# Retention attention into a routed expert layer: expert 0's token list read in place of a replicated one, and half of each gate's first step moved one tile earlier

## The chip, the cores and the metric

The kernel runs on one core of a Trainium2 chip. The metric is the device time of one execution in microseconds (us), and lower is better. A core has five engines that run side by side, each its own instruction queue in order: TensorE (PE in the profile; PEld is its weight loads), VectorE (DVE), ScalarE (ACT), GpSimd (POOL) and SyncE (SP). SyncE here only issues transfers; GpSimd issues the indirect ones (gather and scatter by a list of row numbers). They wait for one another, and for transfers (DMA), through semaphores.

## The reference

Retention attention over 8 batches of 8 heads, 576 positions and head size 64, without a softmax; its output, one row of 512 numbers for each of 4608 tokens, goes through a layer of 8 experts, of which each token uses the one with the largest logit:

```python
scores = scale * np.matmul(q, k.transpose(0, 1, 3, 2))
Dmat = np.where(rel >= 0, gamma[:, None, None] ** rel[None, :, :], 0.0)
ret = np.matmul(scores * Dmat[None], v)
x = ret.transpose(0, 2, 1, 3).reshape(B * S, H * D)

logits = x @ w_gate
e_idx = np.argmax(logits, axis=1)
gate_w = softmax(logits)[np.arange(N), e_idx]
eom = 1.0 / (1.0 + np.exp(-(x @ w_output_gate)))
for e in range(E):
    mask = e_idx == e
    h = np.maximum(x[mask] @ w1[e], 0.0)
    out[mask] = gate_w[mask, None] * eom[mask, e, None] * (h @ w2[e])
```

## The kernel before

**Order.** The whole program stands under a hand-made schedule: each engine executes its instructions in the order in which the Python code issues them. An operation that is written earlier stands earlier in its engine's queue, and everything behind it on that engine waits while it waits. Only the semaphores join the engines.

**The loop** runs over 36 tiles `g` of 128 tokens (nine make two batches). For a tile, `scores(g + 1)` makes the next tile's products of q and k on TensorE, and VectorE masks them into `S_sb` (two operations of 128x512, line 389). `out_x(g)` adds the carried state's part (line 416) and the tile's own part (line 420) into the PSUM tile `o_ps`, of which there is one. From it ScalarE copies `xT` (line 428), x with the features on the partitions, and `x_rows(g)` on VectorE (line 437) transposes x into rows, which SyncE stores to `xs` in DRAM two tiles later (`store_x`). So the next tile's `out_x` cannot begin before `x_rows` has emptied `o_ps`. `update` carries the state on (line 402), `k_rows` transposes k (line 363). GpSimd scales q and v (`prep_q`, `prep_v`, lines 351 and 356), and SyncE loads the packed q, k and v (`pk`) five tiles ahead.

**The gate** runs once for four tiles; `n` numbers these groups, `late` is the tile's place behind its group, 0 to 3. At the end of the tile of late 0, `logits` (line 448) makes the group's logits on TensorE. In the next tile (late 1) `gate_a` finds each token's expert with eight operations on VectorE (a transposition, line 454, and seven small ones up to line 475), ahead of that tile's `out_x` and `x_rows`. At late 2, `ranks` on TensorE and `gate_b` on VectorE turn this into a slot in the expert's list, with `gate_d` (the rounding to `sli`, line 512) at the tile's end; at late 3 `gate_c` makes the list's entries (`meta`, lines 527 to 532), and over the next tiles GpSimd scatters them (`some`, line 536), 64 bytes for each token (its number and its weight) into the list `lst` in DRAM. The last group's gate runs after the loop.

**The experts** follow the loop. Expert `e` takes up to 616 tokens in two parts (`NS` = 360 and 256). `mm1(e, part, fb)` makes one block of 128 hidden features (12 products: the three of a split into high and low halves, by four blocks of 128 input features, line 250), `mm2(e, t)` one tile of output rows (line 266). Weights are split into a high half by ScalarE (`upper`, line 160) and a low half by VectorE (`lower`, line 165).

**Lists.** `load_idx` brings an expert's list entries into SBUF, each of them four times, for the four groups of 32 partitions. `make_idx` on VectorE makes two things from that: `gidx`, row numbers for gathers of quarter rows (line 307), and `idx`, row number and weight for whole rows (four copies, line 311). Part 0 of expert 0 is special: its list is taken from the first 24 tiles' tokens (`SNAP` = 5 is the last group counted), loaded at the end of tile 29, and its rows are gathered in tiles 31 and 32 (`gather_rows`, line 199, into a free `pk` buffer), transposed on TensorE in tile 34 (line 229), and split at tile 35, so that `mm1(0, 0, 0)` starts right behind the loop. The lines of the loop that hold this:

```python
        if g == 31:
            make_idx(0, 2, 0)
        if g + 1 < NTILE:
            prep_v(g + 1)
        if 30 < g < 33:
            for t in (0, 1) if g == 31 else (2,):
                gather_rows(t)
```

Of the kernel before, what the change touches and what calls it, by code (L numbers as in the profile page):

```python
# [38 lines left out]
GT = 4  # L39
NG = NTILE // GT  # L40
# [7 lines left out]
LW, LE = 16, 640  # L48
# [3 lines left out]
def tile_retention_moe(  # L52
# [42 lines left out]
    bump = const.tile([P, 2], F32, name="bump")  # L95
    toks = const.tile([P, NTILE, 1], I32, name="toks")
    meta = [const.tile([P, GT, LW], I32, name=f"meta{i}") for i in range(2)]
    lists0 = const.tile([P, 2, TA * 4, LW], I32, name="lists0")
    idx = const.tile([P, E, CT, 2], I32, name="idx")
    gidx = const.tile([P, E, CT * 4], I32, name="gidx")  # L100
    quad = csm_sb[:, 16:17]
# [56 lines left out]
    def upper(which, e, fp, st):  # L158
        hi = w_of(which, f"w{which}h{fp}")
        A.copy(out=hi, in_=st)  # L160
        return which, e, fp, st, hi
# [28 lines left out]
    def gather_rows(t, dep=None):  # L190

        if t == 0:
            rows = ld.tile([P, 3, 512], F32, name="pk")
            for i in range(TA):
                XG[0, i] = rows[:, i]
# [3 lines left out]
        after(G.indirect_dma_start(out=XG[0, t], out_offset=None, in_=xs[0:n, :],  # L199
                                   in_offset=bass.IndirectOffsetOnAxis(ap=idx[:, 0, t, 0:1], axis=0),  # L200
                                   bounds_check=n - 1, oob_is_err=False), dep)

    def where(t):
        part = 0 if t < TA else 1
        t0 = t - part * TA
        return part, P * t0, min(P, NS[part] - P * t0)

    def xt_of(e, part):
        if (e, part) not in XT:
# [3 lines left out]
        return XT[e, part]  # L213

    def split_x(e, t, src):
        part, c0, n = where(t)
# [10 lines left out]
    def transp_pe(t, src):  # L227
        for k in range(KB):
            T.transpose(src[:, k, :], XG[0, t][:, P * k:P * k + P], ident)
        return split_x(0, t, src)  # L230

    def transp(e, t):
# [23 lines left out]
        return done  # L256

    def mm2(e, t, between={}):
        part, c0, n = where(t)
# [11 lines left out]
        A.activation(out=y, in_=ps, func=AF.Copy, scale=idx.bitcast(F32)[0:n, e, t, 1:2])  # L271
        G.indirect_dma_start(out=out, out_offset=bass.IndirectOffsetOnAxis(ap=idx[0:n, e, t, 0:1], axis=0),  # L272
                             in_=y, in_offset=None, bounds_check=NT - 1, oob_is_err=False)

    lists1 = []

    def load_idx(e0, e1, part):
        s0, t0, nb = part * NS[0], part * 4 * TA, NB[part]

        rest = NS[part] > 32 * nb  # L280
        lists = lists0 if (e0, part) == (0, 0) else lists1[0]
        view = lst[0:E * NT, :].rearrange("(e a s) w -> e a s w", e=E, a=1)
        dmas = []
        if e1 - e0 < 4:

            for e in range(e0, e1):
                v = view[e, :, s0:s0 + 32 * nb].rearrange("a (j t) w -> a j (t w)", t=nb).broadcast_to([4, 32, LW * nb])
                dmas.append(SP.dma_start(out=lists[:, e, t0:t0 + nb].rearrange("p t w -> p (t w)"), in_=v))
                if rest:
                    v = view[e, :, s0 + 32 * nb:s0 + 32 * nb + 32].broadcast_to([4, 32, LW])  # L290
                    dmas.append(SP.dma_start(out=lists[:, e, t0 + nb], in_=v))
        for a in range(4):
            if e1 - e0 >= 4:
                v = view[e0:e1, 0, s0:s0 + 32 * nb].rearrange("e (j t) w -> j e (t w)", t=nb)
                dmas.append(SP.dma_start(out=lists[32 * a:32 * a + 32, e0:e1, t0:t0 + nb].rearrange("j e t w -> j e (t w)"),
                                         in_=v))
                if rest:
                    v = view[e0:e1, 0, s0 + 32 * nb:s0 + 32 * nb + 32].rearrange("e j w -> j e w")
                    dmas.append(SP.dma_start(out=lists[32 * a:32 * a + 32, e0:e1, t0 + nb], in_=v))
        for i in dmas:  # L300
            for j in scat:
                tc.add_manual_dep(i.ins, j.name, SYNC, reason="reads the list after every scatter so far")

    def make_idx(e0, e1, part):
        n, t0 = (TA, 0) if part == 0 else (CT - TA, TA)
        lists = lists0 if (e0, part) == (0, 0) else lists1[0]
        V.tensor_scalar(out=gidx[:, e0:e1, 4 * t0:4 * (t0 + n)], in0=lists[:, e0:e1, 4 * t0:4 * (t0 + n), 0],
                        scalar1=4.0, scalar2=quad, op0=ALU.mult, op1=ALU.add)
        for a in range(4):
            q = slice(32 * a, 32 * a + 32)  # L310
            V.tensor_copy(idx[q, e0:e1, t0:t0 + n],
                          lists[q, e0:e1].rearrange("j e (t u) w -> j e t u w", u=4)[:, :, t0:t0 + n, a, 0:2])
# [131 lines left out]
    def logits(n, ps):  # L444

        for k in range(KB):
            for q in range(GT):
                T.matmul(ps[32 * q:32 * q + 32, 0:P], lhsT=wg_sb[:, k, :], rhs=xT[n][:, q, k, :],
                         start=(k == 0), stop=(k == KB - 1), skip_group_check=True)

    def gate_a(n):
# [116 lines left out]
    for g in range(NTILE):  # L568
# [313 lines left out]
```

## Time and profile before

| what | us |
|---|---|
| median of 3 runs | 605.94 (604.21 to 612.22) |
| the profiled execution | 606.38 |
| its span, first to last instruction | 604.6 |
| TensorE busy | 576.1 (95% of the span) |
| VectorE, GpSimd, ScalarE busy | 327.7, 315.6, 169.7 |

The loop takes the span's first 155 us or so, and the experts the rest. A row of the timeline has the start, the duration, the engine, the line of the kernel, the operation, what it writes and from what, its shape, how many instructions stand in it, and in brackets how long the engine was idle before it and what released it. In the windows the columns are the length, busy time of the five engines with their instruction counts, the granted TensorE clock as a share of the full one, the share of the 16 DMA engines' time in use, and GB/s. A row of the waits has the engine, what it was to run, what it waited for, and the time: in total, how often, and the longest. The releaser is inferred: it is the last of the things waited for that left an event.

TensorE's busy time in the loop by periods of four tiles, from one gate's first `x_rows` to the next one's:

```profile
31.70:47.35 15.65, 15.01 (x354) 12.62 (x346) 10.98 (x32) 5.56 (x15) 10.63 (x13) 1.00 0.99 317
47.35:62.85 15.50, 14.80 (x375) 12.75 (x373) 10.96 (x32) 5.68 (x14) 13.55 (x17) 1.00 0.92 277
...
92.91:108.31 15.40, 15.29 (x395) 13.47 (x396) 11.08 (x32) 6.49 (x17) 13.53 (x17) 1.00 0.90 285
108.31:125.10 16.79, 15.09 (x341) 12.28 (x339) 11.07 (x35) 4.96 (x13) 14.06 (x19) 1.00 0.85 260
```

### The profile page before, as it was taken

The numbers are of one execution on the slowest core, as the hardware profiler recorded it, in microseconds if no ns is written. First come the engines' busy times: TensorE is split into PE (matmuls) and PEld (weight loads), VectorE is DVE, ScalarE is ACT, GpSimd is POOL, SyncE is SP. The second block draws the span as 40 slices with busy tenths as digits, with TensorE's granted clock in tenths as the row PEclk, the third lists the DMA queues.
The fourth block names the chain that finished last, engine by engine and source line by source line (L and its number), as shares of the span: only waits on it lengthen the run. The fifth ranks groups of instructions, "written<-read, shape, count | busy, mean of one in ns | idle before, by whom it ended". The sixth has DMA issues, their size and how long they took to land. (4 is left out here: it accounts for less than half of the span.)

```text
span 604.6 us, 14060 instructions
## 1 busy us (share of the span) xinstructions
PE 576.1 (95%) x5737; PEld 507.2 (84%) x5737; DVE 327.7 (54%) x655; ACT 169.7 (28%) x360; POOL 315.6 (52%) x333
## 2 busy tenths in 40 slices
PE   7999999888798999999999999999999999999995
PEld 4888888777696889779978997998899799889974
DVE  3566777674661869736732961584186249426300
ACT  5434334333341222132212221222222222212210
POOL 4768898867276734363553455446344535540011
PEclk9999999998999999999999999999999999999998
DMA  8999899877646436323621642262155216321001
GB/s 304 297 321 287 275 277 292 250 212 237 175 116 214 123 127 225 93 89 114 200 98 58 192 149 75 81 232 96 48 179 165 82 53 218 118 68 52 1 36 44
DMA packets 53324, 94.78 MB, mean 157 GB/s; under 512 B 9018, under 2 KB 30971, under 8 KB 53258
## 3 DMA queue, kind: packets, MB, share of 16 engines
q1 hardware_dynamic: 43594, 73.03, 38.2%
q0 software_dynamic: 9232, 20.23, 10.3%
q8 instruction: 46, 0.75, 0.5%
q10 hardware_dynamic: 432, 0.59, 0.3%
q14 instruction: 20, 0.16, 0.1%
HBM read 74.33 MB, written 20.15 MB: 156 GB/s over the span
## 5 line engine op out<-in xcount | busy, mean ns | idle before, releaser
L186 POOL DMA_INDIRECT x_q<-xs,gidx x140 | 148.7, 1062 | 113.2 <-ACT hh L254 70.9
L250 PE MATMUL h_ps<-xh,w1h 128*128 128x360 f32 (+1 forms) x512 | 154.6, 302 | 2.6 <-issue 1.3
L250 PE MATMUL h_ps<-xl,w1h 128*128 128x360 f32 (+1 forms) x512 | 154.6, 302 | 0.3 <-issue 0.3
L250 PE MATMUL h_ps<-xh,w1l 128*128 128x360 f32 (+1 forms) x512 | 154.5, 302 | 0.0
L266 PE MATMUL y_ps<-w2h,hh 128*128 128x512 f32 (+1 forms) x320 | 125.2, 391 | 2.4 <-ACT y L271 1.4
L266 PE MATMUL y_ps<-w2h,hl 128*128 128x512 f32 (+1 forms) x320 | 124.9, 390 | 0.5 <-DVE hl L255 0.5
L266 PE MATMUL y_ps<-w2l,hh 128*128 128x512 f32 (+1 forms) x320 | 124.8, 390 | 0.0
L272 POOL DMA_INDIRECT out_dram<-y,idx x40 | 41.1, 1028 | 122.6 <-ACT y L271 111.9
L250 PEld LDWEIGHTS h_ps<-xh,w1h 128*128 128x128 f32 x512 | 96.1, 188 | 3.5 <-issue 1.8
L250 PEld LDWEIGHTS h_ps<-xh,w1l 128*128 128x128 f32 x512 | 97.1, 190 | 0.2 <-issue 0.2
L250 PEld LDWEIGHTS h_ps<-xl,w1h 128*128 128x128 f32 x512 | 96.1, 188 | 1.1 <-issue 0.5
L254 ACT ACTIVATE hh<-h_ps 128x360 fp32r<-128x360 f32 (+1 forms) x128 | 54.5, 429 | 149.5 <-PE h_ps L250 126.6
L255 DVE SCALAR_TENSOR_TENSOR hl<-h_ps,hh 128x360 fp32r<-128x360 f32 (+1 forms) x128 | 58.6, 474 | 69.0 <-ACT hh L254 58.2
L266 PEld LDWEIGHTS y_ps<-w2h,hh 128*128 128x128 f32 (+1 forms) x320 | 58.8, 184 | 16.6 <-ACT y L271 1.8
L266 PEld LDWEIGHTS y_ps<-w2h,hl 128*128 128x128 f32 (+1 forms) x320 | 58.8, 184 | 15.3 <-DVE hl L255 1.3
L266 PEld LDWEIGHTS y_ps<-w2l,hh 128*128 128x128 f32 (+1 forms) x320 | 58.8, 184 | 13.4
L271 ACT ACTIVATE y<-y_ps,idx 128x512 f32<-128x512 f32 (+1 forms) x40 | 27.5, 689 | 129.7 <-issue 75.3
L389 DVE TENSOR_TENSOR S_sb<-sc,cmat_sb 128x512 f32<-128x512 f32 x72 | 46.1, 681 | 32.2 <-PE sc L385 29.6
L223 DVE TENSOR_TENSOR xl<-x_t,xh 128x512 fp32r<-128x512 f32 (+1 forms) x35 | 23.5, 672 | 63.9 <-ACT xh L220 61.9
L351 POOL TENSOR_TENSOR qs<-pk,gq_sb 128x512 f32<-128x512 f32 x36 | 46.2, 1282 | 13.4 <-DMA pk<-in_pack_dram 6.6
L536 POOL DMA_INDIRECT lst<-meta,sli x36 | 36.1, 1004 | 27.1 <-DVE meta L532 15.6
L420 PE MATMUL o_ps<-S_sb,vs 128*64 128x128 f32 x576 | 40.4, 281 | 1.8 <-DVE xq L437 0.7
(126 smaller groups left out, 604.3 us busy)
## 6 DMA issues: line engine op xcount, KB each, us to landing
st<-in_w_dram SPq DMA_DIRECT2D x61, 512.0 KB
pk<-in_pack_dram SPq DMA_DIRECT2D x31, 512.0 KB
pk<-in_pack_dram SPq DMA_DIRECT2D x35, 256.0 KB
xs<-xq SPq DMA_DIRECT2D x40, 128.0 KB
pk<-in_pack_dram SPq DMA_DIRECT2D x3, 768.0 KB
x_q<-xs,gidx POOLq DMA_INDIRECT x140
xs<-w2h SPq DMA_DIRECT2D x16, 128.0 KB
xs<-w2l SPq DMA_DIRECT2D x16, 128.0 KB
```

Source lines behind the costliest of these rows:

```text
L186: after(G.indirect_dma_start(out=XG[e, t][:, u, :], out_offset=None, in_=xs.rearrange("t (a c) -> (t a) c", a=4), in_offset=bass.IndirectO ...
L223: V.tensor_tensor(out=lo, in0=src[:, :, 0:n], in1=hi.bitcast(F32), op=ALU.subtract)
L250: T.matmul(ps, lhsT=a[:, k, :], rhs=b[:, k, :], start=(j == 0), stop=(j == 3 * KB - 1))
L254: done = A.activation(out=hh, in_=ps, func=AF.Relu)
L255: V.scalar_tensor_tensor(out=hl, in0=ps, scalar=0.0, in1=hh.bitcast(F32), op0=ALU.max, op1=ALU.subtract)
L266: i = T.matmul(ps, lhsT=a[:, c0:c0 + n], rhs=b, start=(j == 0), stop=(j == 3 * FB - 1))
L271: A.activation(out=y, in_=ps, func=AF.Copy, scale=idx.bitcast(F32)[0:n, e, t, 1:2])
L272: G.indirect_dma_start(out=out, out_offset=bass.IndirectOffsetOnAxis(ap=idx[0:n, e, t, 0:1], axis=0), in_=y, in_offset=None, bounds_check= ...
L351: G.tensor_tensor(out=qs[g], in0=pk[g][:, 0].rearrange("p (n i) -> p n i", n=NP), in1=gq_sb[:, c % 5], op=ALU.mult)
L389: V.tensor_tensor(out=S_sb[:, r].rearrange("p (a b) i -> p a b i", a=2), in0=sc[r].rearrange("p (a b) i -> p a b i", a=2), in1=m, op=ALU.mult)
L420: last = T.matmul(part(p, r), lhsT=vs[g][:, 2 * p + r, :], rhs=S_sb[:, r, p, :], start=(state is None and p < 2), stop=True, skip_group_ch ...
L536: i = G.indirect_dma_start(out=lst, out_offset=bass.IndirectOffsetOnAxis(ap=sli[:, t, :], axis=0), in_=m[:, t, :], in_offset=None)
```

## The change

1. **Expert 0's list.** `load_rows(part)` brings the list of expert 0 as it lies in DRAM: one transfer in which each partition gets the entries of its own rows. The rows' numbers and weights are used where they lie (`entry`), without an operation on VectorE. Part 0's three tiles hold 120 rows each (`N0`) instead of 128, 128 and 104, so that 360 entries divide evenly. `make_idx(0, 2, 0)` goes from tile 31, and `make_idx(0, 2, 1)` from the experts.
2. **Gathers.** Tile 31 issues one of the three gathers, tile 32 the other two; before it was two and one.
3. **Expert 1's list**, which was loaded beside expert 0's, is loaded at the end of tile 32; its `make_idx(1, 2, 0)` follows the loop, before `mm1(0, 0, 3)`. The remaining lists are loaded and made in other groups: `load_idx(1, E, 1)`, `load_idx(2, E, 0)`.
4. **The gate.** `gate_a`'s first four operations follow `logits` at the end of the tile of late 0; the other four (`gate_e`) stay where all eight were.
5. **Weight casts.** Of the first expert's four casts of w1 on ScalarE, one stands at the end of tile 33 and three after the loop; before, tiles 33, 34 and 35 had one each and one came after the loop.

On VectorE, at a gate inside the loop (group 6, tiles 28 and 29; the others are alike), before; `S_sb` is the masked scores, `lg_ps` the gate's PSUM tile, and L437 is `x_rows`:

```order
L437 STREAM_TRANSPOSE w2h_2310<-o_ps 128x4x4x32
L389 TENSOR_TENSOR S_sb<-sc_132,cmat_sb 128x512
L389 TENSOR_TENSOR S_sb<-sc_133,cmat_sb 128x512
L454 STREAM_TRANSPOSE lg_ps<-lg_ps 128x128
L458 TENSOR_REDUCE mx<-lg_ps 128x4
L459 TENSOR_TENSOR lg_ps<-lg_ps,mx 128x32
L461 TENSOR_TENSOR lm<-lg_ps,mx 128x32
L462 TENSOR_TENSOR lg_ps<-lg_ps,csm_sb 128x32
L464 TENSOR_REDUCE m_2381<-lg_ps 128x4
L470 TENSOR_TENSOR oh<-lg_ps,m_2381 128x32
L475 TENSOR_REDUCE oh<-oh 128x8
L437 STREAM_TRANSPOSE w2h_2310<-o_ps 128x4x4x32
```

And the same place now, where the line numbers have moved (L399 is `S_sb`, L447 `x_rows`):

```order
L447 STREAM_TRANSPOSE w2h_2312<-o_ps 128x4x4x32
L464 STREAM_TRANSPOSE lg_ps<-lg_ps 128x128
L468 TENSOR_REDUCE mx<-lg_ps 128x4
L469 TENSOR_TENSOR lg_ps<-lg_ps,mx 128x32
L471 TENSOR_TENSOR lm<-lg_ps,mx 128x32
L399 TENSOR_TENSOR S_sb<-sc_134,cmat_sb 128x512
L399 TENSOR_TENSOR S_sb<-sc_135,cmat_sb 128x512
L477 TENSOR_TENSOR lg_ps<-lg_ps,csm_sb 128x32
L479 TENSOR_REDUCE m_2383<-lg_ps 128x4
L485 TENSOR_TENSOR oh<-lg_ps,m_2383 128x32
L490 TENSOR_REDUCE oh<-oh 128x8
L447 STREAM_TRANSPOSE w2h_2312<-o_ps 128x4x4x32
```

The four operations up to the one that writes `lm` now stand ahead of the pair that makes `S_sb`.

On VectorE at tile 31, before (`meta` is the list entries of group 6, `gidx` and `idx` what `make_idx` writes):

```order
L531 RECIPROCAL meta_87<-lg_ps 128x4
L532 COPY meta_87<-toks 128x4
L307 TENSOR_SCALAR gidx<-lists_89,csm_sb 128x2x12
L311 COPY idx<-lists_89 32x2x6 x4
L437 STREAM_TRANSPOSE w2l_2484<-o_ps 128x4x4x32
```

Now L437's successor follows the copy to `meta` directly. On GpSimd the gathers stood in tiles 31 and 32 so:

```order
L356 TENSOR_TENSOR vs<-pk,gk_sb 128x512
L199 DMA pk<-xs,idx 128x512 x2
L351 TENSOR_TENSOR qs<-pk,gq_sb 128x512
L356 TENSOR_TENSOR vs<-pk,gk_sb 128x512
L199 DMA pk<-xs,idx 128x512
L351 TENSOR_TENSOR qs<-pk,gq_sb 128x512
```

and stand now so, with `rows` in the place of `idx`:

```order
L366 TENSOR_TENSOR vs<-pk,gk_sb 128x512
L201 DMA pk<-xs,rows_90 120x512
L361 TENSOR_TENSOR qs<-pk,gq_sb 128x512
L366 TENSOR_TENSOR vs<-pk,gk_sb 128x512
L201 DMA pk<-xs,rows_90 120x512 x2
L361 TENSOR_TENSOR qs<-pk,gq_sb 128x512
```

One gather has moved behind the scaling of q for tile 34 and of v for tile 33.

The diff, cut to its core:

```diff
+N0 = 120
...
-    lists0 = const.tile([P, 2, TA * 4, LW], I32, name="lists0")
+    lists0 = const.tile([P, 1, TA * 4, LW], I32, name="lists0")
+    rows0 = [const.tile([P, n, LW], I32, name=f"rows{i}") for i, n in enumerate((TA, CT - TA))]
...
-                                   in_offset=bass.IndirectOffsetOnAxis(ap=idx[:, 0, t, 0:1], axis=0),
+                                   in_offset=bass.IndirectOffsetOnAxis(ap=entry(0, t)[:, 0:1], axis=0),
...
+    def entry(e, t):
+        part, _, n = where(e, t)
+        return idx[0:n, e, t] if e else rows0[part][0:n, t - part * TA]
...
+    def load_rows(part):
+        n = where(0, part * TA)[2]
+        v = lst[part * NS[0]:part * NS[0] + NS[part], :].rearrange("(p t) w -> p (t w)", p=n)
+        read_after(SP.dma_start(out=rows0[part][0:n].rearrange("p t w -> p (t w)"), in_=v))
...
         V.tensor_tensor(out=lm, in0=l, in1=bc(mx), op=ALU.subtract)
+        gt["fst"] = fst
+
+    def gate_e(n):
+        fst, lm = gt["fst"], gt["lm"]
+        bc = lambda a: a.broadcast_to([P, GT, E])
         V.tensor_tensor(out=fst, in0=fst, in1=desc.broadcast_to([P, GT, E]), op=ALU.mult)
...
-        if g == 31:
-            make_idx(0, 2, 0)
...
-            for t in (0, 1) if g == 31 else (2,):
+            for t in (0,) if g == 31 else (1, 2):
                 gather_rows(t)
...
-        if 32 < g < 35:
-            low.append(upper(*wl.pop(0)))
         if n >= 0 and 0 < late < 3:
-            (gate_a, gate_b)[late - 1](n)
+            (gate_e, gate_b)[late - 1](n)
         if g == 35:
...
-            low.append(upper(*wl.pop(0)))
             gate_c(n)
...
             logits(n, gt["ps"])
+            gate_a(n)
...
         if g == 29:
-            load_idx(0, 2, 0)
+            load_rows(0)
+        if g == 32:
+            load_idx(1, 2, 0)
+        if g == 33:
+            low.append(upper(*wl.pop(0)))
...
+    low += [upper(*wl.pop(0)) for _ in range(2)]
...
-    load_idx(0, 2, 1)
+    make_idx(1, 2, 0)
+    load_rows(1)
+    load_idx(1, E, 1)
     load_idx(2, E, 0)
-    load_idx(2, E, 1)
...
-    make_idx(0, 2, 1)
...
+    make_idx(1, E, 1)
     make_idx(2, E, 0)
-    make_idx(2, E, 1)
```

More of the change, by code (lines that the diff above doesn't have):

```diff
@@ L194, in gather_rows @@
             for i in range(TA):
-                XG[0, i] = rows[:, i]
+                XG[0, i] = rows[0:N0, i]
         elif t >= TA:
@@ L199, in gather_rows, with where @@
         after(G.indirect_dma_start(out=XG[0, t], out_offset=None, in_=xs[0:n, :],
-                                   in_offset=bass.IndirectOffsetOnAxis(ap=idx[:, 0, t, 0:1], axis=0),
+                                   in_offset=bass.IndirectOffsetOnAxis(ap=entry(0, t)[:, 0:1], axis=0),
                                    bounds_check=n - 1, oob_is_err=False), dep)
-    def where(t):
+    def where(e, t):
         part = 0 if t < TA else 1
-        t0 = t - part * TA
-        return part, P * t0, min(P, NS[part] - P * t0)
+        t0, w = t - part * TA, P if e or part else N0
+        return part, w * t0, min(w, NS[part] - w * t0)
+    def entry(e, t):
+        part, _, n = where(e, t)
+        return idx[0:n, e, t] if e else rows0[part][0:n, t - part * TA]
     def xt_of(e, part):
@@ L215, in split_x @@
     def split_x(e, t, src):
-        part, c0, n = where(t)
+        part, c0, n = where(e, t)
         hi, lo = (a[:, :, c0:c0 + n] for a in xt_of(e, part))
@@ L227, in transp_pe @@
     def transp_pe(t, src):
+        n = where(0, t)[2]
         for k in range(KB):
-            T.transpose(src[:, k, :], XG[0, t][:, P * k:P * k + P], ident)
+            T.transpose(src[:, k, 0:n], XG[0, t][:, P * k:P * k + P], ident[0:n, 0:n])
         return split_x(0, t, src)
@@ L258, in mm2 @@
     def mm2(e, t, between={}):
-        part, c0, n = where(t)
+        part, c0, n = where(e, t)
         ps = pools["ps_y"].tile([P, DM], F32, name="y_ps")[0:n]
@@ L270, in mm2 @@
         y = pools["y"].tile([P, DM], F32, name="y")[0:n]
-        A.activation(out=y, in_=ps, func=AF.Copy, scale=idx.bitcast(F32)[0:n, e, t, 1:2])
-        G.indirect_dma_start(out=out, out_offset=bass.IndirectOffsetOnAxis(ap=idx[0:n, e, t, 0:1], axis=0),
+        A.activation(out=y, in_=ps, func=AF.Copy, scale=entry(e, t).bitcast(F32)[:, 1:2])
+        G.indirect_dma_start(out=out, out_offset=bass.IndirectOffsetOnAxis(ap=entry(e, t)[:, 0:1], axis=0),
                              in_=y, in_offset=None, bounds_check=NT - 1, oob_is_err=False)
     lists1 = []
+    def load_rows(part):
+        n = where(0, part * TA)[2]
+        v = lst[part * NS[0]:part * NS[0] + NS[part], :].rearrange("(p t) w -> p (t w)", p=n)
+        read_after(SP.dma_start(out=rows0[part][0:n].rearrange("p t w -> p (t w)"), in_=v))
     def load_idx(e0, e1, part):
@@ L280, in load_idx @@
         rest = NS[part] > 32 * nb
-        lists = lists0 if (e0, part) == (0, 0) else lists1[0]
+        early = (e0, part) == (1, 0)
         view = lst[0:E * NT, :].rearrange("(e a s) w -> e a s w", e=E, a=1)
[L283 to L299, printed above, removed]
@@ L300, in load_idx @@
-        for i in dmas:
-            for j in scat:
-                tc.add_manual_dep(i.ins, j.name, SYNC, reason="reads the list after every scatter so far")
+        if early:
+            v = view[1, :, s0:s0 + 32 * nb].rearrange("a (j t) w -> a j (t w)", t=nb).broadcast_to([4, 32, LW * nb])
+            read_after(SP.dma_start(out=lists0[:, 0, t0:t0 + nb].rearrange("p t w -> p (t w)"), in_=v))
+            v = view[1, :, s0 + 32 * nb:s0 + 32 * nb + 32].broadcast_to([4, 32, LW])
+            read_after(SP.dma_start(out=lists0[:, 0, t0 + nb], in_=v))
@@ new lines, in load_idx, with read_after @@
+        for a in () if early else range(4):
+            q = slice(32 * a, 32 * a + 32)
+            v = view[e0:e1, 0, s0:s0 + 32 * nb].rearrange("e (j t) w -> j e (t w)", t=nb)
+            read_after(SP.dma_start(out=lists1[0][q, e0:e1, t0:t0 + nb].rearrange("j e t w -> j e (t w)"), in_=v))
+            if rest:
+                v = view[e0:e1, 0, s0 + 32 * nb:s0 + 32 * nb + 32].rearrange("e j w -> j e w")
+                read_after(SP.dma_start(out=lists1[0][q, e0:e1, t0 + nb], in_=v))
+    def read_after(i):
+        for j in scat:
+            tc.add_manual_dep(i.ins, j.name, SYNC, reason="reads the list after every scatter so far")
@@ L304, in make_idx @@
     def make_idx(e0, e1, part):
         n, t0 = (TA, 0) if part == 0 else (CT - TA, TA)
-        lists = lists0 if (e0, part) == (0, 0) else lists1[0]
-        V.tensor_scalar(out=gidx[:, e0:e1, 4 * t0:4 * (t0 + n)], in0=lists[:, e0:e1, 4 * t0:4 * (t0 + n), 0],
+        lists = lists0 if (e0, part) == (1, 0) else lists1[0][:, e0:e1]
+        V.tensor_scalar(out=gidx[:, e0:e1, 4 * t0:4 * (t0 + n)], in0=lists[:, :, 4 * t0:4 * (t0 + n), 0],
                         scalar1=4.0, scalar2=quad, op0=ALU.mult, op1=ALU.add)
@@ L311, in make_idx @@
             V.tensor_copy(idx[q, e0:e1, t0:t0 + n],
-                          lists[q, e0:e1].rearrange("j e (t u) w -> j e t u w", u=4)[:, :, t0:t0 + n, a, 0:2])
+                          lists[q].rearrange("j e (t u) w -> j e t u w", u=4)[:, :, t0:t0 + n, a, 0:2])
     actx = ExitStack()
@@ L459, in gate_a @@
         V.tensor_tensor(out=fst, in0=l, in1=bc(mx), op=ALU.is_equal)
-        lm = sm.tile([P, GT, E], F32, name="lm")
+        lm = gt["lm"] = sm.tile([P, GT, E], F32, name="lm")
         V.tensor_tensor(out=lm, in0=l, in1=bc(mx), op=ALU.subtract)
+        gt["fst"] = fst
+    def gate_e(n):
+        fst, lm = gt["fst"], gt["lm"]
+        bc = lambda a: a.broadcast_to([P, GT, E])
         V.tensor_tensor(out=fst, in0=fst, in1=desc.broadcast_to([P, GT, E]), op=ALU.mult)
@@ L639, in tile_retention_moe @@
     gt["ps"] = ps_1.tile([P, 512], F32, name="lg_ps")
-    mm1(0, 0, 0, {5: lambda: (logits(NG - 1, gt["ps"]), gate_a(NG - 1))})
+    mm1(0, 0, 0, {5: lambda: (logits(NG - 1, gt["ps"]), gate_a(NG - 1), gate_e(NG - 1))})
     mm1(0, 0, 1, {9: lambda: ranks(NG - 1)})
```

## The prediction

> **What bounds the kernel now.** I read the page's head first, then busy time by stretches of 20 us, then what TensorE waited for, then the timeline around the longest waits.
>
> ```profile
> span 604.6 us, 14060 instructions
> ...
> PEclk9999999998999999999999999999999999999998
> ```
>
> ```profile
> 20.00:40.00 20.00, 19.50 (x502) 16.80 (x501) 13.70 (x36) 8.26 (x20) 12.88 (x14) 1.00 0.99 308
> ...
> 120.00:140.00 20.00, 17.28 (x401) 14.80 (x390) 11.84 (x37) 7.16 (x17) 13.49 (x14) 0.91 0.79 252
> ```
>
> In the columns (length, PE, PEld, DVE, ACT, POOL, clock, DMA share, GB/s) TensorE is nearly full from 20 to 40 us, and loses much towards the loop's end: 2.7 us idle from 120 to 140, with the clock at 0.91. The change acts only up to about 180 us, so the sum is over the idle time of TensorE up to there. First the waits in 20 to 128, then those in 128 to 165:
>
> ```profile
> PE o_ps L416 <- DVE xq L437: 1.2, 2, 0.7
> PE o_ps L416 <- DVE w2h L437: 1.1, 2, 0.6
> PE o_ps L420 <- DVE xq L437: 0.7, 1, 0.7
> PE o_ps L420 <- DVE sli L512: 0.6, 1, 0.6
> ```
>
> ```profile
> PE o_ps L416 <- DVE w2l L437: 2.2, 1, 2.2
> ...
> PE o_ps L416 <- DVE sli L512: 1.7, 1, 1.7
> ```
>
> L437 is x_rows, the transposition that empties o_ps, which the next tile's out_x (L416) writes. So VectorE being late with x_rows costs 3.0 us in steady running, 0.6 at the step behind it, and 2.2 us once at tile 31.
>
> **The change, term A: the list at tile 31.**
>
> ```profile
> 131.38 0.14 DVE L532 COPY meta<-toks 128x4 int32<-128x4 int32 x1
> ...
> 131.76 0.90 PE L385 MATMUL sc<-qs,pk 64*64 64x128 f32 x32
> ...
> 133.16 0.24 DVE L307 TENSOR_SCALAR gidx<-lists,csm_sb 128x24 int32<-128x24 int32 x1 [1.64 <-DMA lists<-lst]
> 133.31 0.69 DVE L311 COPY idx<-lists 32x12 int32<-32x12 int32 x4
> ...
> 134.04 0.72 DVE L437 STREAM_TRANSPOSE w2l<-o_ps 128x512 f32<-128x512 f32 x1
> ...
> 134.90 0.67 PE L416 MATMUL o_ps<-qs,stT 64*64 64x128 f32 x16 [2.24 <-DVE w2l L437]
> 134.91 1.07 POOL L199 DMA_INDIRECT pk<-xs,idx  x1 [5.61 <-DMA xs<-w2h]
> ```
>
> VectorE stands 1.64 us for the list's DMAs, then spends 0.9 us on make_idx, and x_rows(31) queues behind both. The change takes all five operations out of this place. x_rows can then start at 131.52, when L532 ends, and end at 132.24, before scores end at 132.66. All 2.24 us go. Bounds: 0 (if x_rows finds another wait) to 2.24; I take 2.2, as nothing stands between L532 and L437 any more.
>
> Behind this idle time the clock falls:
>
> ```profile
> 136.10:139.50 3.40, 3.40 (x46) 2.90 (x46) 0.72 (x1) 1.43 (x4) 3.19 (x3) 0.50 1.06 395
> ```
>
> ```profile
> 159.40:161.60 2.20, 0.07 (x2) 0.00 (x1) 1.52 (x8) 0.30 (x1) 1.07 (x2) 1.00 0.78 260
> 161.60:165.00 3.40, 3.40 (x25) 3.40 (x25) 2.70 (x6) 0.76 (x3) 0.00 (x0) 1.00 0.06 20
> ```
>
> For 3.40 us it is 0.50, so 1.7 us of work are lost. If the idle time caused it, it goes with it: 1.7; if not, it stays: 0. I take 1.7, since no other fortieth of the span but the last has a clock below 9 tenths (PEclk, above), and it comes right behind the span's longest gap. But the almost equal gap at 159.4 (0.07 us busy of 2.20) is followed by a clock of 1.00. [...]
>
> **Gathers and queues.** On SyncE four list DMAs become one of 23 KB, at the same place; two others (expert 1) move to the end of tile 32:
>
> ```profile
> 127.67 0.65 SPq L288 DMA_DIRECT2D lists<-lst  x1
> ...
> 129.56 0.54 SPq L291 DMA_DIRECT2D lists<-lst  x1
> ```
>
> The loads behind them go out 1.8 us sooner, and those behind tile 32 about 1.2 us later; TensorE waits for neither kind (no pk or weight load stands among its waits): 0. If that cover went, 1.2.
> Gather 0 needs no VectorE and goes at about 132 instead of 134.91. (The releaser in its row had long landed; it needs idx, which L311 left at 134.02.) The second moves from tile 31 to 32, behind qs and vs, as the third was:
>
> ```profile
> 137.32 1.28 POOL L351 TENSOR_TENSOR qs<-pk,gq_sb 128x512 f32<-128x512 f32 x1
> 138.55 1.05 POOL L356 TENSOR_TENSOR vs<-pk,gk_sb 128x512 f32<-128x512 f32 x1
> 139.76 1.04 POOL L199 DMA_INDIRECT pk<-xs,idx  x1 [0.16 <-issue]
> ...
> 181.31 1.00 POOL L199 DMA_INDIRECT x_q<-xs,idx  x1 [0.31 <-issue]
> ```
>
> ```profile
> 147.48 0.67 PE L229 MATMUL kt<-ident,pk 128*128 128x128 f32 x4
> ...
> 188.79 0.63 PE L229 MATMUL t_ps<-ident,x_q 128*128 128x128 f32 x4 [0.18 <-DMA x_q<-xs,idx]
> ```
>
> From 132 on, 1.07, 1.28, 1.05, two gathers of 1.04 and gaps of some 0.2 give 138.1 for the end of the third; it was 140.8. Its four transposes stand behind eight others (0.67 for four), began near 148.9, and begin at about 145 with TensorE 4 us ahead: 6.8 us behind the end of the gather's instruction. The one gather whose landing the trace shows to be waited for took 188.79 − 182.31 = 6.5 us. Slack 0.3 us: cost 0, bounds 0 to 1.
>
> **Term B: four operations of each gate.**
>
> ```profile
> 103.26 1.08 PE L448 MATMUL lg_ps<-xT,wg_sb 128*32 128x128 f32 x32
> ...
> 104.28 0.90 PE L385 MATMUL sc<-qs,pk 64*64 64x128 f32 x32
> ...
> 105.24 1.29 DVE L389 TENSOR_TENSOR S_sb<-sc,cmat_sb 128x512 f32<-128x512 f32 x2 [1.57 <-PE sc L385]
> ...
> 106.44 0.32 DVE L454 STREAM_TRANSPOSE lg_ps<-lg_ps 128x128 f32<-128x128 f32 x1
> ...
> 108.31 0.70 DVE L437 STREAM_TRANSPOSE xq<-o_ps 128x512 f32<-128x512 f32 x1
> ...
> 109.16 0.67 PE L416 MATMUL o_ps<-qs,stT 64*64 64x128 f32 x16 [0.55 <-DVE xq L437]
> ```
>
> All eight take 108.31 − 106.44 = 1.87 us; the first of them is 0.32 long and the others are near 0.2, so I give the first four 1.04. The change puts them into the 1.57 us in which VectorE waits for scores: logits end at 104.34, so the four end at 105.38 and delay S_sb by 0.14. x_rows comes 1.04 − 0.14 = 0.9 us sooner, more than the longest of the waits (0.7). Eight gates lie in the loop. All of the four waits listed (3.6 us) may go: the one behind `sli` too, since the S_sb pair and gate_b queue behind the later x_rows. A stall that goes lets TensorE run into the next limit: from 20 to 40 us the DMA share is already 0.99. I take 3.0; bounds 0 to 3.6 (a loss is a rival below).
>
> **Term C: weight casts on ScalarE.**
>
> ```profile
> 152.73 1.08 ACT L160 CAST w1h<-st 128x1024 fp32r<-128x1024 f32 x1
> ```
>
> ```profile
> 151.97 1.09 PE L420 MATMUL o_ps<-S_sb,vs 128*64 128x128 f32 x16
> 154.31 0.40 PE L250 MATMUL h_ps<-xh,w1h 128*128 128x360 f32 x1 [1.25 <-ACT xT L428]
> ```
>
> ```profile
> 169.86 1.23 DVE L165 TENSOR_TENSOR w2l<-w2h,w2h 128x1024 fp32r<-128x1024 f32 x1 [0.40 <-ACT w2h L160]
> ```
>
> xT(35) queued behind this cast, and the first mm1 product waited 1.25 us for it. Without the cast it starts when out_x(35) is done, at 153.06, 0.6 us sooner (bounds 0 to 1.2). The three casts of 1.08 now follow the loop; the pair they serve is needed two feature blocks of 12 products later, 0. make_idx for expert 1 (0.93 us) moves behind the loop, into mm1, where VectorE waits for ScalarE's w2 casts (169.86 is the first of several): 0, and 0.9 without that cover. Tiles of 120 instead of 128, 128 and 104 rows leave the number of products and their 360 columns as they are: 0.
>
> **Sum.** 2.2 + 1.7 + 3.0 + 0.6 = 7.5 us. The profiled execution took 606.38 (span 604.6); 606.38 − 7.5 = 598.9, told as 599. The median of the runs, 605.94, lies 0.4 below that execution, so this is 1.2% under the median. A measurement of this kernel tells about 2% (12 us) from no change.
>
> **The rivals.**
> *Only the end of the loop pays.* If DMA or POOL sets the loop's pace (DMA share 0.99 early, against it: TensorE never waits for a load after 20 us), term B is taken up by later waits: 606.4 − 4.5 = 601.9.
> *The clock step stays or moves to another gap,* for which the clean gap at 159.4 speaks: 600.6.
> *More goes.* The 1.7 us wait behind `sli` and part of the idle stretch at 159.4 come from VectorE and ScalarE seeing TensorE's results late:
>
> ```profile
> 155.55 1.08 PE L448 MATMUL lg_ps<-xT,wg_sb 128*32 128x128 f32 x32
> ```
>
> ```profile
> 159.84 0.33 DVE L454 STREAM_TRANSPOSE lg_ps<-lg_ps 128x128 f32<-128x128 f32 x1 [2.82 <-remote]
> ```
>
> These logits end at 156.63, and VectorE starts on them 3.2 us later; I can't say why. If the cast moved off ScalarE or the sooner gathers end one of these, 1.7 to 2.1 more go: 597.
> *Nothing is gained: the gathers become the wait.* Each us that the third lands later than 6.8 us after its instruction is one us; at 11 us terms A and C are eaten: 603 to 606.
> *Slower: late logits block VectorE.* The four operations now stand ahead of S_sb. If the lag of 3.2 us held at every gate, S_sb would start 3.2 + 0.14 us late, and x_rows 3.34 − 1.04 = 2.3 later than before; times 8 gates is 18.4, less A and C 4.5: 620. It decides from a lag of 0.9 us a gate (no gain there), and 1.5 us eats the rest. Against it: at 105.24 S_sb starts 0.06 us after scores end (104.28 + 0.90), with no such lag.
>
> **How the numbers follow.** Forecast 599: 0.45. Only the loop's end, 602: 0.22. Clock step stays, 600.6: 0.10. More goes, 597 and under: 0.13. Gathers wait, 603 to 606: 0.06. Late logits, 610 and over: 0.04. The range runs from 595 (all upper bounds, 2.24 + 1.7 + 3.6 + 1.2, and 2 us more) to 604 and leaves out about 1 in 10. Faster by over 2% would need under 594, beyond all upper bounds: 0.04. Slower by over 2%: 0.03. Within 2%: 0.93.
>
> **What would show it.** A: no wait of PE for L437 at tile 31, a clock of 1.00 there, gather 0 at about 132. B: the waits for L437 gone between 20 and 128, S_sb within 0.3 us of scores. C: the first mm1 product less than 0.8 us after out_x(35). Wrong would be the forecast if the periods of four tiles stayed at their length though these waits were gone, or if L229 waited for a DMA.

## The result, and the profile after

| kernel | median, us | runs | ratio to before (95% interval) |
|---|---|---|---|
| before | 609.24 (604.21 to 614.52) | 20 | |
| after | 602.40 (597.26 to 608.91) | 20 | 0.9889 (0.9865 to 0.9914) |

The change makes the kernel 1.1% faster; 1.2% was forecast. The range of 595 to 604 holds the median. Over 20 executions the kernel before came out at 609.24, about 3 us above the execution of 606.38 that the forecast subtracts from; 7.5 us less than 609.24 is 601.7. Here and below a ratio leaves out executions over 1.5% slower than the fastest, and it need not be the quotient of the two medians. The two profiled executions differ by less than the medians do (spans 604.6 and 602.3 us), so the profile after has to be read with care: it shows what the change removed, and also a loss that not every execution has.

Busy time of after by stretches of 20 us (the columns as before: PE, PEld, DVE, ACT, POOL, clock, DMA share, GB/s):

```profile
20.00:40.00 20.00, 19.71 (x511) 17.13 (x511) 13.73 (x36) 8.88 (x21) 12.15 (x12) 1.00 0.96 291
...
120.00:140.00 20.00, 19.23 (x466) 16.07 (x457) 12.81 (x37) 6.52 (x17) 16.51 (x17) 1.00 0.83 263
140.00:160.00 20.00, 13.68 (x203) 11.38 (x199) 12.11 (x35) 8.70 (x16) 10.02 (x17) 0.93 0.74 211
160.00:180.00 20.00, 20.00 (x101) 18.65 (x100) 13.22 (x29) 7.66 (x14) 11.21 (x13) 0.90 0.43 113
```

From 120 to 140 the half clock is gone and TensorE is busy 2 us more. It now stands idle for 6.3 of the 20 us from 140 to 160, and part of the time from there to 180 runs at half clock. The timeline of after at tile 31 (line numbers have moved: L447 is x_rows, L399 S_sb, L426 and L430 out_x, L201 the gathers):

```profile
130.61 0.14 DVE L547 COPY meta<-toks 128x4 int32<-128x4 int32 x1
130.67 0.72 DVE L447 STREAM_TRANSPOSE w2l<-o_ps 128x512 f32<-128x512 f32 x1
...
130.99 0.90 PE L395 MATMUL sc<-qs,pk 64*64 64x128 f32 x32
131.38 1.12 POOL L201 DMA_INDIRECT pk<-xs,rows  x1 [2.54 <-PE kt L373]
131.71 0.65 PE L426 MATMUL o_ps<-qs,stT 64*64 64x128 f32 x16
```

x_rows(31) follows the copy to meta at once, and out_x(32) starts behind scores without a wait. What TensorE waited for between 20 and 128 us:

```profile
PE o_ps L426 <- issue: 0.8, 2, 0.5
PE lg_ps L458 <- issue: 0.6, 1, 0.6
...
PE o_ps L430 <- DVE sli L527: 0.4, 1, 0.4
PE o_ps L426 <- DVE xq L447: 0.2, 1, 0.2
```

Of 3.0 us behind x_rows 0.2 are left. What replaced them in part is "issue": TensorE idle while it waited for nothing that the profile shows, 2.4 us in all rows of 20 to 128, where it was 0.7 before. x_rows(4) started at 26.35 before and 27.10 after, x_rows(30) at 128.31 and 127.54, x_rows(31) at 134.04 and 130.67, x_rows(35) at 155.21 and 149.09; the first mm1 product at 154.31 and 148.03. So the loop ends 6.3 us sooner. Counted from x_rows(4), which started 0.75 us later, it is 7.0 us shorter up to the first mm1 product: 1.5 us up to x_rows(30), and 5.5 us from there. Then after loses 4 of the 6.3 us in this execution:

```profile
150.64 0.28 PE L458 MATMUL lg_ps<-xT,wg_sb 128*32 128x128 f32 x1 [0.42 <-issue]
...
157.21 0.33 DVE L464 STREAM_TRANSPOSE lg_ps<-lg_ps 128x128 f32<-128x128 f32 x1 [5.95 <-remote]
...
158.97 0.19 PE L501 MATMUL lg_ps<-oh,cbf_sb 128*128 128x32 bf16 x1 [4.37 <-DVE oh L485]
```

The last group's logits end at 150.92, VectorE starts on them 6.3 us later, and TensorE, which has gone on with mm1, waits 4.37 us at `ranks` (L501) for the result. In the two other profiles of after, below, it waits there 0.8 us and not at all. Behind the gap of 4.37 us the clock is 0.50 for 5.2 us, longer than the 3.40 us of the profile before:

```profile
158.90:164.10 5.20, 5.13 (x22) 5.13 (x22) 3.59 (x13) 0.86 (x4) 0.00 (x0) 0.50 0.08 24
```

One more wait is new in after, and it is the change's own:

```profile
135.44 0.66 SPq L299 DMA_DIRECT2D lists<-lst  x1
136.14 0.57 SPq L301 DMA_DIRECT2D lists<-lst  x1
...
144.63 1.06 POOL L551 DMA_INDIRECT lst<-meta,sli  x1 [4.81 <-PE kt L237]
145.73 1.23 POOL L366 TENSOR_TENSOR vs<-pk,gk_sb 128x512 f32<-128x512 f32 x1
...
147.01 1.09 PE L430 MATMUL o_ps<-S_sb,vs 128*64 128x128 f32 x16 [1.07 <-POOL tick L550]
```

The list of expert 1 is read from `lst` at the end of tile 32. The scatter of tile 33 writes into `lst` and, in the program, waits until that read is done. It stands 4.81 us on GpSimd (the releaser named is only the last event seen), v of tile 35 is scaled behind it, and out_x(35) waits 1.07 us.

### The profile page after: what moved, and what is told of

The parts are those of the page before. It is cut to its first block, busy times and chain, and to the rows that moved or that the text cites. A ratio compares the mean times of both kernels' runs of the same rounds, so it can differ in the third digit from the quotient of the medians.

```text
span 602.3 us, 14063 instructions
## 1 busy us (share of the span) xinstructions
PE 578.3 (96%) x5737; PEld 509.5 (85%) x5737; DVE 327.2 (54%) x650; ACT 170.4 (28%) x360; POOL 313.1 (52%) x333
## 5 line engine op out<-in xcount | busy, mean ns | idle before, releaser
L188 POOL DMA_INDIRECT x_q<-xs,gidx x140 | 145.4, 1038 | 115.4 <-ACT hh L262 74.0
L274 PE MATMUL y_ps<-w2h,hh 128*128 128x512 f32 (+2 forms) x320 | 125.3, 392 | 1.6 <-ACT y L279 1.4
L274 PE MATMUL y_ps<-w2l,hh 128*128 128x512 f32 (+2 forms) x320 | 124.9, 390 | 0.0
L274 PE MATMUL y_ps<-w2h,hl 128*128 128x512 f32 (+2 forms) x320 | 124.9, 390 | 0.0
L280 POOL DMA_INDIRECT out_dram<-y,idx x35 | 35.6, 1017 | 116.2 <-ACT y L279 105.9
L274 PEld LDWEIGHTS y_ps<-w2h,hh 128*128 128x128 f32 (+2 forms) x320 | 58.8, 184 | 16.1 <-ACT y L279 1.8
L274 PEld LDWEIGHTS y_ps<-w2h,hl 128*128 128x128 f32 (+2 forms) x320 | 58.8, 184 | 14.5 <-DVE hl L263 0.4
L274 PEld LDWEIGHTS y_ps<-w2l,hh 128*128 128x128 f32 (+2 forms) x320 | 58.8, 184 | 13.5
L399 DVE TENSOR_TENSOR S_sb<-sc,cmat_sb 128x512 f32<-128x512 f32 x72 | 46.2, 683 | 23.6 <-PE sc L395 19.6
L279 ACT ACTIVATE y<-y_ps,idx 128x512 f32<-128x512 f32 (+1 forms) x35 | 24.1, 689 | 118.5 <-issue 67.1
L430 PE MATMUL o_ps<-S_sb,vs 128*64 128x128 f32 x576 | 40.4, 279 | 2.1 <-POOL tick L550 1.1
```

What stands on the lines that cost most here:

```text
L188: after(G.indirect_dma_start(out=XG[e, t][:, u, :], out_offset=None, in_=xs.rearrange("t (a c) -> (t a) c", a=4), in_offset=bass.IndirectO ...
L279: A.activation(out=y, in_=ps, func=AF.Copy, scale=entry(e, t).bitcast(F32)[:, 1:2])
L399: V.tensor_tensor(out=S_sb[:, r].rearrange("p (a b) i -> p a b i", a=2), in0=sc[r].rearrange("p (a b) i -> p a b i", a=2), in1=m, op=ALU.mult)
L430: last = T.matmul(part(p, r), lhsT=vs[g][:, 2 * p + r, :], rhs=S_sb[:, r, p, :], start=(state is None and p < 2), stop=True, skip_group_ch ...
```

## The experiments

The kernels ran in three sets of four, each set on one chip with the kernel before beside it. The chips differ: before has a median of 597.5, 610.1 and 597.8 us on them. The first and the third are called the faster chips below; the second, and that of the result above, the slower ones.

| run | set | median, us | ratio to before (95% interval) |
|---|---|---|---|
| list and gathers alone | 1 | 594.52 | 0.9958 (0.9937 to 0.9979) |
| gate alone | 1 | 596.31 | 0.9972 (0.9948 to 0.9995) |
| casts alone | 1 | 598.38 | 1.0011 (0.9989 to 1.0033) |
| after, ranks one block later | 1 | 591.88 | 0.9930 (0.9902 to 0.9958) |
| after | 2 | 602.69 | 0.9898 (0.9865 to 0.9931) |
| after, list 1 at tile 30 | 2 | 603.05 | 0.9912 (0.9877 to 0.9947) |
| the same, ranks one block later | 2 | 602.38 | 0.9907 (0.9871 to 0.9944) |
| the same, all gathers at tile 32 | 2 | 601.74 | 0.9898 (0.9846 to 0.9950) |
| after | 3 | 593.80 | 0.9918 (0.9887 to 0.9950) |
| after, list 1 at tile 30 | 3 | 590.02 | 0.9882 (0.9835 to 0.9930) |
| the same, gate's eight operations together | 3 | 593.57 | 0.9928 (0.9889 to 0.9966) |
| before with filler products | 3 | 597.61 | 0.9993 (0.9961 to 1.0025) |

**List and gathers alone.** After, with the gate and the casts put back (the lines of the gate; those of the casts are left out here):

```diff
+            if late == 1:
+                gate_a(n)
             (gate_e, gate_b)[late - 1](n)
...
-            gate_a(n)
...
```

> Only the list and the gathers are changed; the gate's eight operations and the weight casts stand as before. By the prediction this is term A: no wait of TensorE behind x_rows at tile 31 (2.2 us) and no half clock there (1.7), so 3.9 us, a ratio of 0.9935 to the kernel before. A rival says that the whole gain of 6.8 us (ratio 0.989) comes from here, since the loop's end is where the traces of before and after part; another that what is gained here is lost again behind the loop, where after shows a gap of 4.4 us, so that the list alone is within 1 us (0.998 to 1.0).

Measured 0.42% (0.2 to 0.6), that is 2.5 us (1.3 to 3.8) of the 3.9. The wait at tile 31 and the half clock there are gone, but the timeline shows a new wait in their place:

```profile
143.53 1.06 POOL L551 DMA_INDIRECT lst<-meta,sli  x1 [5.31 <-DVE w1l L167]
144.63 1.05 POOL L366 TENSOR_TENSOR vs<-pk,gk_sb 128x512 f32<-128x512 f32 x1
...
145.73 1.92 PE L430 MATMUL o_ps<-S_sb,vs 128*64 128x128 f32 x16 [2.44 <-POOL tick L550]
```

Sixteen products that took 1.09 us elsewhere take 1.92: right behind the 2.44 us of idle time the clock is halved for 3.4 us, one place further on.

**The gate alone**, in the kernel before (the split of `gate_a` in two is left out here):

```diff
             logits(n, gt["ps"])
+            gate_a(n)
...
-            (gate_a, gate_b)[late - 1](n)
+            (gate_e, gate_b)[late - 1](n)
```

> Only the gate's first four operations are moved; list and casts stand as before. By the prediction 3.0 us, a ratio of 0.995. By the trace of after, where the waits behind x_rows went but x_rows of tile 30 came only 1.5 us sooner than before against that of tile 4, it is 1.5 us: 0.9975. If the lag of late logits decides, it is 1.0 or above.

Measured 0.28% (0.05 to 0.5), 1.7 us. No wait for L437 is left between 20 and 128 us. From x_rows(4) to x_rows(30) the loop takes 95.4 us; with the list alone it takes 100.2, with the casts alone 101.7. But at tile 31 TensorE waits longer than in the profile before:

```profile
123.50 0.65 SPq L288 DMA_DIRECT2D lists<-lst  x1
...
128.83 0.24 DVE L307 TENSOR_SCALAR gidx<-lists,csm_sb 128x24 int32<-128x24 int32 x1 [3.86 <-DMA lists<-lst]
...
130.57 1.13 PE L416 MATMUL o_ps<-qs,stT 64*64 64x128 f32 x16 [4.47 <-DVE w2l L437]
```

The gap is 4.47 us, twice that of the profile before. The moved gate isn't the reason, for with the casts alone, where the gate stands as before, it is as long:

```profile
135.27 0.24 DVE L307 TENSOR_SCALAR gidx<-lists,csm_sb 128x24 int32<-128x24 int32 x1 [4.04 <-DMA lists<-lst]
...
137.01 1.13 PE L416 MATMUL o_ps<-qs,stT 64*64 64x128 f32 x16 [4.64 <-DVE w2l L437]
```

What differs is when the list is asked for. VectorE uses it 5.49 us after the first of its four loads went out in the profile before, and 5.33 us after it with the gate alone. That load goes out 0.64 us before x_rows(30) in the profile before and 1.7 us after it with the gate alone. VectorE's use of the list follows x_rows(30) by 4.85 us in the profile before, 7.07 with the gate alone and 7.26 with the casts alone. Why SyncE comes to it later on this chip isn't shown.

**The casts alone**: the casts of tiles 33, 34 and 35 at the places that they have in after.

> Only the weight casts are moved. By the prediction 0.6 us: 0.999. If a cast ahead of xT(34) was the cause of the late stretch from 147 to 151 us (which after does not show), 2.5 us: 0.996.

No gain: 1.0011 (0.9989 to 1.0033). The interval still allows 0.6 us; the 2.5 us are excluded. The wait has only changed hands: the first mm1 product no longer waits for ScalarE's xT, but 0.92 us for VectorE's low half of x (line 223).

**Ranks one block later**, in after:

```diff
-    mm1(0, 0, 1, {9: lambda: ranks(NG - 1)})
+    mm1(0, 0, 1)
+    mm1(0, 0, 2, {9: lambda: ranks(NG - 1)})
...
-    mm1(0, 0, 2)
```

> After, with the last group's ranks one feature block of mm1 later (12 products, 2 us), so that TensorE does not reach them before VectorE has the experts of the last group. If the gap of 4.4 us there and the half clock behind it cost what the profile of after shows, about 2 us of the gap and the 2.4 us of the half clock go: ratio to before 0.982 instead of 0.989. If the gap only moves to the next thing that waits for the last group's gate (the scatters, the gathers of part 1 and their transposition), the ratio stays at 0.989 or worse.

0.9930 on this chip, where after itself was not run; the third set has after at 0.9918 on a chip with the same time before. Nothing was gained that can be measured, and the profiles say why: in after's profile of the third set `ranks` does not wait either (the logits end at 150.65, `ranks` follows at 153.32).

**After again, and expert 1's list earlier.** The second is one move:

```diff
-        if g == 32:
-            load_idx(1, 2, 0)
+        if g == 30:
+            load_idx(1, 2, 0)
```

> The changed kernel again, beside the variants below on one chip. Forecast as before: ratio 0.989. If the three parts only add up as measured alone (0.9958, 0.9972, 1.0011), 0.994.

> After, with the list of expert 1 loaded at the end of tile 30 instead of tile 32. In after, the scatter of tile 33 writes the same lst and waits until that load has read it (POOL idle 4.8 us), v of tile 35 is scaled behind it, and out_x(35) waits (1.1 us in after, 2.4 in list-only, both for POOL). If so, the POOL idle falls under 1.5 us, PE no longer waits for POOL at the second half of out_x(35), and the time falls by 1 to 2 us against after (ratio to after 0.997). If another transfer holds the scatter, nothing changes.

> The changed kernel a third time, beside the three below. 0.989 if the gain is that of the first two measurements; 0.993 to 0.995 if this chip is like the one on which the parts were measured (the kernel before near 597 us, no late signals, no idle time put down to issue).

> After with the list of expert 1 loaded at tile 30, again. On a chip like the one of the parts, where the wait of out_x(35) for POOL was 2.1 to 2.4 us with 3.4 us of half clock behind it (1.7 us lost), 2 to 4 us below after: 0.994 to 0.997 of after. On a chip like the one of the second set, where TensorE was late there anyway: no difference.

On the second set's chip the move changed nothing (602.69 and 603.05), though GpSimd's wait went (2.62 us, now 0.16); TensorE had no wait for POOL there even in after, and with the move out_x(35) waits 2.14 us for ScalarE's copy of the state. On the third set's chip it gave 3.8 us by the medians (593.80 and 590.02) and 2.2 us by the ratios, whose intervals overlap (0.9887 to 0.9950, 0.9835 to 0.9930): with six runs of one and twelve of the other the size is known only as 0 to 5 us. What the profiles show is clearer. There after has the wait, with the half clock behind it (1.98 us for the sixteen products):

```profile
143.81 1.06 POOL L551 DMA_INDIRECT lst<-meta,sli  x1 [4.67 <-DVE w1l L167]
144.91 1.04 POOL L366 TENSOR_TENSOR vs<-pk,gk_sb 128x512 f32<-128x512 f32 x1
...
146.01 1.98 PE L430 MATMUL o_ps<-S_sb,vs 128*64 128x128 f32 x16 [2.08 <-POOL tick L550]
```

and with the list at tile 30 the scatter goes at once, v of tile 35 is ready early, and what is left is the third gather:

```profile
136.09 1.06 POOL L551 DMA_INDIRECT lst<-meta,sli  x1 [0.17 <-issue]
137.19 1.04 POOL L366 TENSOR_TENSOR vs<-pk,gk_sb 128x512 f32<-128x512 f32 x1
...
140.71 0.60 PE L237 MATMUL sc<-ident,pk 120*128 120x120 f32 x4 [1.56 <-DMA pk<-xs,rows]
141.24 0.67 PE L426 MATMUL o_ps<-qs,stT 64*64 64x128 f32 x16
141.84 1.09 PE L430 MATMUL o_ps<-S_sb,vs 128*64 128x128 f32 x16
```

**Two more variants** on the second set's chip, the list at tile 30 with `ranks` one block later, and the same with all gathers at tile 32 (`if g == 32: for t in range(TA)`):

> The same with the last group's ranks one block of mm1 later. If the gap at ranks is a cost of each execution, 2 to 4 us below the run with the list at tile 30; if it is met only in some executions, 0 to 1.5 us.

> The same again with all three gathers at tile 32, so that q of tile 34 and v of tile 33 are not queued behind a gather that still waits for its list on POOL (1.5 us idle there, and a wait of 0.9 us of PE for qs, in the run with ranks one block later). If POOL's order is the limit there: 0.5 to 1 us below the run before it, and no wait of PE for qs. If the gathers' landing decides instead, PE waits longer at the transpositions (L237; 0.5 us there) and the time is the same or 1 us above.

Both within the noise of after (0.9907, 0.9898). The wait at `ranks` fell from 2.2 us to 0.6 with the later `ranks`, and the time did not follow measurably. The last one could not decide its question on this chip: TensorE has no wait for qs or for the gathers of part 0 in it, but it has none in the run beside it either. In its profile TensorE gets its own instructions in portions:

```profile
135.32 0.36 PE L412 MATMUL st_ps<-vs,kn 128*64 128x64 f32 x4 [0.40 <-issue]
136.06 0.35 PE L412 MATMUL st_ps<-vs,kn 128*64 128x64 f32 x5 [0.38 <-issue]
136.79 0.36 PE L412 MATMUL st_ps<-vs,kn 128*64 128x64 f32 x5 [0.38 <-issue]
```

Four or five products, then 0.4 us of nothing, every 0.73 us; the profile names no other engine as the cause.

**The whole gate, with the list at tile 30**: the list at tile 30, and the gate as in the kernel before.

> The same as the run beside it, but with the gate's eight operations together at the tile of late 1, as in the kernel before. The difference is what the moved four are worth once the list no longer stops TensorE at tile 31: 3.0 us by the prediction's term B, 1.7 us by the run with the gate alone, where what was gained was waited for again at tile 31 (4.5 us there instead of 2.2). If the waits behind x_rows come back (3 us and more between 20 and 128) and the time is up by less than 1 us, something else sets the loop's pace.

593.57 against 590.02: 3.5 us by the medians, 2.7 by the ratios (nine runs against six, so again some 0 to 5 us). The waits of TensorE between 20 and 128 us are back (those behind L447 sum to 3.4):

```profile
PE o_ps L426 <- DVE w2h L447: 1.3, 3, 0.6
PE o_ps L426 <- DVE xq L447: 1.2, 2, 0.7
PE o_ps L430 <- DVE xq L447: 0.7, 1, 0.7
...
PE o_ps L426 <- DVE w2l L447: 0.2, 1, 0.2
```

With the four operations moved, only the last of these rows was left.

**Filler products.** The kernel before, with products that nobody reads in the gap of tile 31:

```diff
+        if g == 32:
+            for _ in range(20):
+                T.matmul(gt["ps"][:, 400:512], lhsT=ident, rhs=ident[:, 0:112], start=True, stop=True,
+                         skip_group_check=True)
         made = out_x(g, S_sb, prev, lambda last: load(g + 5, 1, last) if g + 5 < NTILE else None)
```

> The kernel before with 20 products of 128x112 on TensorE, which nobody reads, ahead of out_x(32), where it waits for x_rows(31). They take about 2.8 us, the wait itself stays. If the idle time makes the clock fall, the half clock behind it (1.7 us lost in before, 3.4 us lost where the wait was 4.5 us) goes or is halved: 1 to 3 us faster than before where the wait is longer than the filler, same where it is shorter. If the clock step is not this gap's, the half clock stays in this place, and the time is the same or up to 0.6 us longer.

```profile
129.66 4.72 PE L612 MATMUL lg_ps<-ident 128*128 128x112 f32 x40
134.31 0.67 PE L416 MATMUL o_ps<-qs,stT 64*64 64x128 f32 x16
```

```profile
134.30:141.00 6.70, 6.70 (x167) 5.84 (x167) 3.46 (x8) 3.02 (x6) 6.19 (x6) 1.00 0.99 338
```

They took 4.72 us, not the 2.8 of the author's estimate (the trace counts 40 of them), and filled the whole wait: scores ended at 129.74 and x_rows(31) at 133.83. Behind it the clock is 1.00; behind waits of that length left empty it was halved (4.47 us with the gate alone: 0.52 over 6.5 us; 4.64 with the casts alone: 0.50 from 135.0 to 141.0). So in these profiles the idle time is the cause. The time did not follow: 0.9993 (0.9961 to 1.0025), at most 2.3 us gained. The half clock behind the empty wait costs 3.1 us of work with the gate alone and 2.2 with the casts alone, and the filler itself may have delayed out_x(32) by up to 0.5 us. The mean clock over the runs rose only from 0.9924 to 0.9948, some 1.4 us of 600: perhaps not every execution of before has the long half clock there. What it costs on average stays open.

## Why the prediction was right

The sum came out, 7.5 us forecast and 6.8 measured, but by terms that are not all those of the sum, and in part by luck: where the parts were measured singly, on other chips, one term wasn't found and a loss came in that the sum puts at 0. On the chips on which the whole was forecast and measured no run separates the terms.

- **Term A, the list at tile 31 (2.2 + 1.7).** The mechanism was right: in every kernel with the new list the wait for L447 at tile 31 and the half clock behind it are gone. With its own new wait out of the way, list and casts together are worth 4.2 us (597.78 to 593.57; interval 2.0 to 6.6), against 3.9 in the forecast. But that isn't the same sum: the gap was 2.24 us in the profile before, and 4.47 and 4.64 on a chip where, with the gate alone, the list was asked for later in the loop (1.7 us after x_rows(30), not 0.64 before it).
- **"TensorE waits for neither kind: 0".** This step failed. I priced the move of expert 1's list as two issues on SyncE and their delay of the loads, and did not ask who waits for the reading of `lst`. The next scatter does, on GpSimd, with v of tile 35 behind it and out_x(35) behind that: 1.07 us in after, 2.08 to 2.44 with 3.4 us of half clock near it (up to 1.7 us of work) on the faster chips. Moving the load two tiles up took both away, and 3.8 us by the medians (2.2 by the ratios) on one chip.
- **Gathers (0, bounds 0 to 1).** The prediction names a wait of L229 for a DMA as a sign of being wrong, and on the faster chips it is there (L237 now): 0.2 to 0.5 us in four profiles and 1.56 in one. The other part was not in the prediction: gather 0, where it stands in tile 31, waits on GpSimd until 2.82 us after its list was asked for in after, and 2.85 in its run of the third set (1.5 to 2.9 us of idle time in the profiles that have it there), and q of tile 34 behind it made TensorE wait 0.2 to 1.3 in four profiles of the faster chips.
- **Term B (3.0).** Right in place. In size it is 1.7 us (0.3 to 3.1) alone, and 3.5 by the medians or 2.7 by the ratios with the list out of the way; these aren't clear of one another, nor of 3.0. On the faster chips the loop's pace shows it: x_rows(4) to x_rows(30) takes 95.4 to 99.7 us in the four kernels with the moved operations and 99.3 to 103.2 in the four without. On the slower chips it doesn't: 102.0 before, and 100.4 to 102.4 in the five with them. There the waits behind x_rows went and others, "issue" among them, came.
- **The rival of late logits**, by which the four operations would block VectorE, did not come up to 128 us: from 20 us on L464 started at most 1.0 us behind its logits. At the gate near 138 us it was 1.5 to 2.2 us in four of the five profiles of the new gate on the slower chips.
- **Term C (0.6).** Not found (1.0011), though its sign is there: in after the first mm1 product (148.03) starts as out_x(35) ends.
- **The rival "only the end of the loop pays"**: its 4.5 us are too few (the interval of the gain is 5.2 to 8.2), but in after's profile part of its picture holds. Only 1.5 of the 7.0 us came before x_rows(30), where term B's waits were, and 5.5 came behind it, where A and C make 4.5. The wait of 1.7 us behind `sli`, which the rival "more goes" names, is gone there too. No run takes these apart on the slower chips.
- **The rival "the clock step moves to another gap"** is what the profile after shows, at `ranks`, and what the list alone shows at out_x(35). I gave it 1 in 10, and 8 of the 14 profiles show 3.4 or 6.8 us of half clock between 90 and 220 us at another place than tile 31.

On the third set's chip the medians give A 4.2, B 3.5 and 3.8 for the new wait. They add up to after's 4.0 of themselves, since they are differences of the same four medians; that is a split and not a check. On the chips with before at 609 to 610 after gains 6.8 and 7.4 by the medians. That fits A and B without the new wait (7.7), and there expert 1's list earlier indeed gains nothing. But the ratios of after on the three chips (0.9889, 0.9898, 0.9918) have intervals that overlap, so it isn't shown that it gains more there.

The best version is the one with expert 1's list at tile 30: 0.9882 against 0.9918 of after on one chip, and no difference on another.

## What to carry to other kernels

A moved load must be priced with those who wait for its reading as well as for its data: a write to the same buffer (here 4.81 us on GpSimd), the queue that this write stands in, and what is behind it there (1.07 to 2.44 us of TensorE). A gap that ends with a transfer should be read in more than one profile: the one at tile 31 was 2.24 us in one and 4.47 in another, where the transfer was asked for later in the loop. And of the 15 idle gaps of TensorE from 2.08 us up (table below) 11 cost more than their length, with 3.4 or 6.8 us of half clock, so a gap taken away in one place is worth its clock only if no other gap of that length comes instead.

## What the runs showed of the hardware

**Idle gaps and the clock.** These are all idle gaps of TensorE over 1.3 us between 90 and 220 us in all 14 profiles, and the half-clock stretches at them:

| gap, us | count | half clock at its end or behind it |
|---|---|---|
| 1.31 to 1.81 | 9 | never |
| 2.08 to 2.44 | 10 | 3.4 us in 6, none in 4 |
| 2.92 to 4.64 | 5 | 6.8 us in each |

The shortest with half clock at it is 2.08 us long (after, third set). At the five gaps of 2.92 us and more the half clock lasts twice as long as at six of the shorter ones, 6.8 us against 3.4, but its first 0.1 to 2.4 us fall into the gap itself, so that it costs 2.2 to 3.3 us of work against 1.5 to 1.7. From 2.08 to 2.44 us the length alone doesn't decide: in both runs of the second set with expert 1's list at tile 30 and two gathers at tile 32, out_x(35) waits 2.14 us, and only the one with the later `ranks` has half clock behind it. One half-clock stretch, at 210 us in the run with all gathers at tile 32, stood behind several shorter gaps (0.97 us the longest).

**The clock and the spread of the times.** A kernel's time and its mean granted clock go together from run to run: over the 26 runs of before in the third set the correlation is −0.80, with 0.6 us for each 0.001 of clock, which is a thousandth of the 600 us (−0.64 and −0.84 in the other two sets). By that slope the clock's range there, 0.987 to 0.998, makes some 7 of the 8 us of spread. What moves the clock from run to run isn't shown: only one execution of each kernel has a profile.

**Late signals on some chips.** In all six profiles from chips with before at 606 to 610 us VectorE waits at least twice for 2.2 to 6.0 us for results of TensorE that by the records had ended before (the rows with "remote"; in before scores end at 115.83 and S_sb starts at 118.15); in all eight from the chips with before near 597.6 it never does. In the same six TensorE gets some five products every 0.73 us at 117 to 119 us, as above. What holds the signals up isn't shown.
